# The attention stage of a fused attention and MoE kernel: its instructions in a hand-written order per pair of heads

## The chip, the cores and the metric

The program runs on 1 core of one Trainium2 chip, in one launch. The metric is the device time of one execution in microseconds (us), here the median of 3 runs; smaller is better.

## What is computed

Attention with a decay, then a mixture of experts with one expert per token, then a gated MLP:

```python
# attention: q, k, v are (4, 8, 576, 64), f is (4, 8, 576)
scores = scale * np.matmul(q, k.transpose(0, 1, 3, 2))
cum = np.cumsum(np.log(np.clip(f, 0.0001, 1.0)), axis=-1)
decay = cum[:, :, :, None] - cum[:, :, None, :]
scores = np.where(causal, -1000000000.0, scores + decay)
attn = np.exp(scores - np.max(scores, axis=-1, keepdims=True))
attn = attn / (np.sum(attn, axis=-1, keepdims=True) + 1e-09)
x = np.matmul(attn, v)                       # -> 2304 tokens of 512
# routing and experts: 8 experts, 512 -> 1024 -> 512
e_idx = np.argmax(x @ w_gate + modality_bias[modality_id], axis=1)
out[mask] = gate_w[mask, None] * (np.maximum(x[mask] @ w1[e], 0.0) @ w2[e])
# gated MLP: 512 -> 1536 -> 512
y = (1.0 / (1.0 + np.exp(-(out @ w_gate2))) * (out @ w_val)) @ w_out
```

## The kernel before

Attention comes first and fills about the first 360 us; behind it follow the end of the routing, the experts and the gated MLP, whose code the change leaves as it is (products at L953 and L963, L1288 and L1376).

**Pairs.** Attention works on 16 pairs: one head of two batches side by side, the two batches j = 0, 1 in the two halves of the arrays. The 576 rows of a head are five blocks of rows, b = 0 (64 rows) and 1 to 4 (128 rows), of which a block needs only the columns up to its diagonal.

**Steps.** `run` goes through steps n = 0 to 17. Step n works on four pairs at once:
- pair n: its scores. QA to QD are the products q·k (L202, in PSUM tiles `s`); T0 to T4 (Ta and Tb are halves of T4) add the decay from `dec` to them, write the sum to the SBUF tiles `sc` and keep each row's minimum in `mn` (L209 on VectorE, DVE for short); E0 to E4 take the exponential in place on ScalarE (ACT) and leave row sums in `sm` (L218).
- pair n−1: X, Y and Z transpose its probabilities on TensorE (PE) into PSUM banks of the tag `t` (L235). A bank holds four to six 128x128 blocks and is copied out whole to `px`, `py` or `pz`, for j = 1 by DVE (L239), for j = 0 by ACT (L241). A0 to A2 and M are the products with v (L291) into `o` and `m`, which are copied to `ot`. `sums` adds 1e-9 to the row sums on GpSimd (POOL, L279, tile `r`) and takes their reciprocal on DVE (L280).
- pair n−2: U takes from a list the two parts of `normalise`: `ot` is transposed back by a product with `iw` (L323, L328; it carries the gate's columns along), scaled by `r` on DVE (L331, L510), and the logits are added up on POOL (L511).
- pair n+1: U also takes `prep`, the transposes of q and k (L174, L180, copied out at L169 by ACT and L167 by DVE); `mask` builds the decay tile `dec` on POOL, ten tensor_scalars (L153) and ten affine_selects (L157). The loads of v for pair n+1, and of q, k and the decay row (`cum`) for pair n+2, are issued on the SP queue.

The banks `t` are two (`TB = 2`) and serve X, Y, Z, `prep` and `normalise`, 12 fills a step; `s` has four, `o` and `m` one each, `dec` two pairs.

**What sets the order.** A tile scheduler reorders the whole program by its own estimates; the string `ORDER` sets only in which order the steps are handed to it. L takes an item from a list of late work (routing of the first half of the tokens, sending `x` to HBM), one or two per step.

Of the kernel before, what the change touches and what calls it, by code (L numbers as in the profile page):

```python
# [20 lines left out]
P = 128  # L21
# [35 lines left out]
    return slice(0, P) if b else slice(D * j, D * (j + 1))  # L57


class Attention:  # L60


    NV = 3
    ORDER = "QA T1 Ta X QB Tb T0 U Y E1 E4 A0 L QC T3 Z E3 A1 U E0 QD T2 U E2 A2 M U U L"

    def __init__(self, tc, ctx, top, ro, ps, q, k, v, f):
        nc = self.nc = tc.nc
# [35 lines left out]
        self.load_v(0)  # L103
        nc.vector.tensor_copy(self.swp[:, 0:64], ident[:, 64:128])
        nc.vector.tensor_copy(self.swp[:, 64:128], ident[:, 0:64])

    def spare(self, tag, shape, dt):

# [36 lines left out]
    def mask(self, n):  # L145

        nc = self.nc
        d = self.dec[n] = [self.pd.tile([P, DW], F32, tag="dec", name="dec") for j in range(2)]
        for b in (1, 4, 0, 3, 2):
            for j, c in enumerate(self.cum[n]):  # L150
                r, m = lanes(b, j), P if b else D
                t = d[j]
                nc.gpsimd.tensor_scalar(  # L153
                    t[r, DO[b]:DO[b] + W[b]], c[r, 0:W[b]], -1.0, c[r, R0[b]:R0[b] + 1], ALU.mult, ALU.add
                )
                sl = t[r, DO[b] + W[b] - m:DO[b] + W[b]]
                nc.gpsimd.affine_select(sl, sl, [[-1, m]], ALU.is_ge, NEG, base=0, channel_multiplier=1)  # L157
        del self.cum[n]

    def prep(self, n):  # L160

        nc, ident = self.nc, self.ident
        qk = self.qk[n] = [self.pt.tile([P, S], F32, tag=t, name=t) for t in ("qT", "qk")]

        def put(w, dst, src):
            if w:
                nc.vector.tensor_copy(dst, src)  # L167
            else:
                nc.scalar.activation(dst, src, AF.Copy, scale=0.125)  # L169

        def main(w):
            t, raw = self.bank(), self.raw[n][w]
            for c in range(4):
                nc.tensor.transpose(t[:, c * P:(c + 1) * P], raw[:, c].rearrange("p j d -> p (j d)"), ident)  # L174
            put(w, qk[w][:, 0:512], t)

        def rest():
            t = self.bank((P, 2, D))
            for w in range(2):
                nc.tensor.transpose(  # L180
                    t[:, w], self.raw[n][w][0:64, 4].rearrange("p j d -> p (j d)"), ident[0:64, 0:64]
                )
            for w in range(2):
                put(w, qk[w][:, 512:576], t[:, w])

        return [lambda: main(0), lambda: main(1), rest]

    def scores(self, n):
        nc = self.nc
        s, d = self.sc[n % 2], self.dec.pop(n)  # L190
        mn = [self.wk.tile([P, 6], F32, tag="mn", name="mn", bufs=4) for j in range(2)]
        q, k = self.qk[n]
        sm = self.sm[n] = self.wk.tile([P, 9], F32, tag="sm", name="sm", bufs=2)
        t = {}

        def qk(items):
# [20 lines left out]
                so, c = s[j][r, SO[b]:SO[b] + W[b]], 2 * (b - 1) + j if b else 8  # L217
                nc.scalar.activation(so, so, AF.Exp, bias=mn[j][r, b:b + 1], scale=-1.0, accum_out=sm[r, c:c + 1])  # L218

        return qk, add_max, exp  # L220

    def probs(self, n):

# [16 lines left out]
            else:  # L240
                nc.scalar.activation(dst, src, AF.Copy)  # L241

        def x():
            for j in range(2):
                t = self.bank()
                for b in (4, 3, 2, 1):
                    tr(j, t[:, P * (b - 1):P * b], b, 0)
                put(j, p[j][0], t)

        def y():  # L250
            for j in range(2):
                t = self.bank()
                tr(j, t[:, 384:512], 0, 0, j == 0)
                tr(j, t[:, 0:128], 1, 1, True)
                for b in (2, 3, 4):
                    tr(j, t[:, 64 + P * (b - 2):64 + P * (b - 1)], b, 1)
                put(j, p[j][1], t)

        def z():
            for j in range(2):  # L260
                t = self.bank()
                tr(j, t[:, 0:128], 3, 3, True)
                tr(j, t[:, 64:192], 4, 3)
                tr(j, t[:, 192:320], 2, 2, True)
                tr(j, t[:, 256:384], 3, 2)
                tr(j, t[:, 384:512], 4, 2)
                put(j, p[j][2][:, 0:512], t)
            t = self.bank((P, 2, P))
            for j in range(2):
                tr(j, t[:, j], 4, 4, True)  # L270
            nc.vector.tensor_copy(pz[:, :, 512:576], t[:, :, 0:64])

        return x, y, z

    def sums(self, n):
        nc, sm = self.nc, self.sm.pop(n)
        r = self.r[n] = self.wk.tile([P, 9, 1], F32, tag="r", name="r", bufs=3)
        rf = r.rearrange("p t o -> p (t o)")
        nc.gpsimd.tensor_scalar(rf, sm, 1e-9, None, ALU.add)  # L279
        nc.vector.reciprocal(rf, rf)  # L280

    def values(self, n):

# [15 lines left out]

        def c2():  # L300
            mm(o[0][:, 192:512], 2, 2, 192, 512, False, False)
            mm(o[0][:, 320:512], 3, 2, 0, 192, False, False)
            mm(o[0][:, 448:512], 4, 2, 512, 576, False, True)
            nc.vector.tensor_copy(ot[:, 64:S], o[0])

        def first():
            om = self.ps.tile([P, 64], F32, tag="m", name="m", bufs=1)
            mm(om, 0, 1, 448, 512, True, True)
            nc.vector.tensor_copy(ot[:, 0:64], om)

        return c0, c1, c2, first

    def normalise(self, n):
        nc = self.nc
# [4 lines left out]
        def part(b0, k, last):  # L319
# [6 lines left out]
                )  # L326
            for j in range(2 * last):
                nc.tensor.matmul(t[D * j:D * (j + 1), 2 * k], ot[:, 0:D], iw[:, h, j], start=True, stop=True)  # L328
            m, t0 = 2 * k + last, 2 * (b0 - 1)
            g, rs = HT * bp + t0, r[:, t0:t0 + m]  # L330
            nc.vector.tensor_tensor(  # L331
# [1 line left out]
            )  # L333
            self.ro.logits(slice(g, g + m), h, t[:, 0:m, D:], rs)

        return [lambda: part(1, 3, 0), lambda: part(4, 1, 1)]

    def run(self):
        N = len(self.pairs)
        nop = lambda *a: None  # L340
        pend, late = [], []

        def unit(todo):
            if todo:
                todo.pop(0)()

        for u in self.prep(0):
            u()
        self.load_dec(0)
        self.mask(0)  # L350
        self.load_qk(1)
        self.load_dec(1)
        n = 0
        while n < N + 2 or pend or late:
            if n == 0:
                self.ro.load()
            if n == 1:
                self.ro.biases()
            if n == 4:
                self.ro.tables()  # L360
            if 2 <= n < N + 2:
                m = n - 2
                pend += self.normalise(m)
            if n + 1 < N:
                self.load_v(n + 1)
                pend[:0] = self.prep(n + 1)
                self.mask(n + 1)
            if n + 2 < N:
                self.load_qk(n + 2)
                self.load_dec(n + 2)  # L370
            qk = add_max = exp = nop
            if n < N:
                qk, add_max, exp = self.scores(n)
            px = py = pz = nop
            av = (nop,) * 4
            if 1 <= n <= N:
                px, py, pz = self.probs(n - 1)
                av = self.values(n - 1)
                self.sums(n - 1)

            step = {
                "QA": lambda: qk([(4, 0, 256, 0), (1, 0, 192, 256)]),
                "QB": lambda: qk([(4, 256, 320, 0), (0, 0, 64, 320)]),
                "QC": lambda: qk([(3, 0, 448, 0)]),
                "QD": lambda: qk([(2, 0, 320, 0)]),
                "Ta": lambda: add_max(4, 0, 256), "Tb": lambda: add_max(4, 256, 576),
                "T0": lambda: add_max(0), "T1": lambda: add_max(1), "T2": lambda: add_max(2), "T3": lambda: add_max(3),
                "E0": lambda: exp(0), "E1": lambda: exp(1), "E2": lambda: exp(2), "E3": lambda: exp(3),
                "E4": lambda: exp(4),
                "X": px, "Y": py, "Z": pz, "A0": av[0], "A1": av[1], "A2": av[2], "M": av[3],  # L390
                "U": lambda: unit(pend), "L": lambda: unit(late),
            }
            for key in self.ORDER.split():
                step[key]()
            if 2 <= n < N + 2 and n % 2:
                late += self.ro.columns(*self.pairs[n - 2])
            n += 1


class Routing:  # L400
# [33 lines left out]
        self.tc = wp.tile([P, 2 * E + 1], F32, tag="tc", name="tc")  # L434
        self.given = mid, w_gate, bias

    def load(self):
        nc, (mid, w_gate, bias) = self.nc, self.given
        nc.gpsimd.memset(self.iw, 0.0)
        for i in range(2):  # L440
            a = slice(D * i, D * (i + 1))
            nc.vector.tensor_copy(self.iw[a, :, i, 0:D], self.ident[a, a].unsqueeze(1).to_broadcast([D, H, D]))
            nc.sync.dma_start(self.iw[a, :, i, D:], w_gate.rearrange("(h p) e -> p h e", p=D))
        for bp in range(2):
            ids = mid.bitcast(I32).rearrange("(b s two) -> b s two", b=B, two=2)
# [1035 lines left out]
def decayed_attention_top1_moe_gated_kernel(  # L1481
# [15 lines left out]
    with ExitStack() as c1:  # L1497
# [4 lines left out]
        with ExitStack() as c0:  # L1502
            with ExitStack() as top:
                att = Attention(tc, c0, top, ro, ps, q, k, v, f)
                att.run()
            ro_t = c1.enter_context(tc.tile_pool(name="ro_t", bufs=1, side="right", reuse_waits="tile"))
            ex.begin(att)
            collect = ro.finish(ro_t, ps)
# [79 lines left out]
```

## Time and profile before

| what | value |
|---|---|
| median of 3 runs | 1054.45 us (1054.3 to 1055.09) |
| profiled execution | 1057.33 us, its span 1055.6 us |
| mean granted clock of TensorE | 0.961 |
| busy share of the span | PE 91%, DVE 67%, ACT 51%, POOL 21% |
| start of step 0's scores | 8.48 us |
| first operation of the second half's argmax (end of attention) | 360.60 us |

The span is the part of an execution that the profiler shows. The busy shares are means over stages with different limits; attention is the first third. The granted clock of TensorE is given in shares of 2.4 GHz; 0.5 is its lower level, 1.2 GHz.

### The profile page before, as it was taken

To read this page: it belongs to the slowest core of one execution; us is meant where nothing else is said; L and a number is where in the kernel's file an instruction comes from. 1 tells how busy PE (TensorE), PEld (TensorE's weight loads), DVE (VectorE), ACT (ScalarE), POOL (GpSimd) and SP (SyncE) were. 2 spreads that over 40 slices of the span, in tenths; PEclk is the share of its full clock that TensorE was granted. 3 is DMA by queue.
4 is the path that set the end of the run, shared out by engine and by line. 5 is a ranking of instruction groups with operands and counts; after the bars stand their busy time and mean duration, and the time that the engine had idled before them with its cause. 6 is when DMAs were issued, how large, how long until landed. Compare 5 with 4: busy or idle time off the path is not lost. (4 is left out here: it accounts for less than half of the span.)

```text
span 1055.6 us, 16303 instructions
## 1 busy us (share of the span) xinstructions
PE 959.2 (91%) x5423; PEld 774.2 (73%) x5423; DVE 705.4 (67%) x1744; ACT 533.4 (51%) x1155; POOL 222.7 (21%) x467
## 2 busy tenths in 40 slices
PE   6796788886789899999999999899999999999996
PEld 3463444443445688999999798789999899999995
DVE  4563434444645597999998747878866688876662
ACT  4443333333335155666667734555665555655452
POOL 6564333444334313111112000000020000200002
PEclk9898889889889999999999989999999999999999
DMA  6452422243621264684578464421332112321201
GB/s 139 119 130 67 103 71 57 68 112 80 193 69 41 48 198 147 220 313 161 170 239 292 157 244 135 146 80 60 120 140 80 60 61 79 111 71 65 76 21 60
DMA packets 118892, 126.69 MB, mean 120 GB/s; under 512 B 65744, under 2 KB 92880, under 8 KB 118800
## 3 DMA queue, kind: packets, MB, share of 16 engines
q1 hardware_dynamic: 114160, 110.87, 34.4%
q0 software_dynamic: 4640, 14.70, 4.1%
q8 instruction: 44, 0.72, 0.3%
q14 instruction: 48, 0.39, 0.1%
HBM read 127.03 MB, written 24.21 MB: 143 GB/s over the span
## 5 line engine op out<-in xcount | busy, mean ns | idle before, releaser
L1288 PE MATMUL g<-x,wc 128*128 128x384 f32 x1536 | 304.6, 340 | 10.0 <-ACT pc L1325 3.1
L1288 PEld LDWEIGHTS g<-x,wc 128*128 128x128 f32 x1536 | 276.3, 189 | 30.1 <-ACT pc L1325 4.4
L1376 PE MATMUL o<-wo,ah 128*128 128x512 f32 x648 | 184.5, 397 | 0.2 <-DVE ah L1313 0.2
L218 ACT ACTIVATE sc<-sc,mn 128x192 f32<-128x192 f32 (+4 forms) x160 | 88.8, 556 | 184.3 <-DVE mn L209 183.8
L1376 PEld LDWEIGHTS o<-wo,ah 128*128 128x128 f32 x648 | 118.0, 188 | 11.6 <-DVE ah L1313 1.0
L153 POOL TENSOR_SCALAR dec<-cum 128x192 f32<-128x192 f32 (+4 forms) x160 | 84.2, 536 | 145.8 <-DVE mn L209 133.2
L1384 POOL DMA_INDIRECT out_dram<-os,tok x18 | 18.4, 1024 | 423.2 <-ACT os L1383 417.7
L887 DVE TENSOR_TENSOR wl<-ws,wh 128x1024 fp32r<-128x1024 f32 x80 | 97.0, 1215 | 0.0
L881 ACT ACTIVATE wh<-ws 128x1024 fp32r<-128x1024 f32 x80 | 84.6, 1060 | 18.6 <-PE y L963 18.6
L1312 ACT ACTIVATE ah<-s 128x384 fp32r<-128x384 f32 x72 | 37.9, 526 | 99.7 <-DVE s L1311 99.7
L235 PE MATMUL t<-swp,sc 128*128 128x128 f32 x144 | 38.9, 322 | 53.9 <-DVE px L239 53.2
L209 DVE CUSTOM_DVE_ANT_0 sc<-s,dec 128x192 f32<-128x192 f32 (+4 forms) x160 | 61.5, 417 | 36.0 <-PE s L202 26.0
L235 PEld LDWEIGHTS t<-swp,sc 128*128 128x128 f32 x144 | 19.9, 157 | 79.7 <-DVE px L239 55.8
L953 PE MATMUL h<-xh,wh 128*128 128x256 f32 x256 | 73.6, 288 | 0.0
L953 PE MATMUL h<-xh,wl 128*128 128x256 f32 x256 | 72.5, 283 | 0.7 <-DVE wl L887 0.7
L202 PE MATMUL s<-qk,qT 64*128 64x320 f32 (+4 forms) x384 | 69.4, 452 | 3.7 <-DVE mn L209 3.1
L953 PE MATMUL h<-xl,wh 128*128 128x256 f32 x256 | 72.4, 283 | 0.3 <-DVE xl L908 0.3
L235 PE MATMUL t<-ident,sc 128*128 128x128 f32 x336 | 64.5, 306 | 1.1 <-ACT px L241 0.7
L933 POOL DMA_INDIRECT rows_by_expert<-ys,dst x20 | 23.9, 1195 | 195.4 <-ACT hh L923 106.0
L235 PEld LDWEIGHTS t<-ident,sc 128*128 128x128 f32 x336 | 45.9, 157 | 25.1 <-ACT sc L218 19.3
L1325 ACT ACTIVATE pc<-g 128x384 f32<-128x384 f32 x96 | 46.4, 483 | 31.1 <-PE g L1288 31.0
L1171 DVE TENSOR_TENSOR wc<-wf,wc 128x512 fp32r<-128x512 f32 x72 | 40.7, 568 | 30.7 <-ACT wc L1168 30.7
(266 smaller groups left out, 1844.2 us busy)
## 6 DMA issues: line engine op xcount, KB each, us to landing
ws<-in_moe_w_dram SPq DMA_DIRECT2D x80, 512.0 KB
wf<-wd SPq DMA_DIRECT2D x36, 512.0 KB
cum<-drow SPq DMA_DIRECT2D x32, 288.0 KB
wd<-dec SPq DMA_DIRECT2D x18, 512.0 KB
wof<-wd SPq DMA_DIRECT2D x18, 512.0 KB
raw<-in_moe_w_gate_dram SPq DMA_DIRECT2D x12, 512.0 KB
raw<-in_moe_w_val_dram SPq DMA_DIRECT2D x12, 512.0 KB
raw<-in_moe_w_out_dram SPq DMA_DIRECT2D x12, 512.0 KB
```

The lines of the kernel that those rows point to most:

```text
L153: nc.gpsimd.tensor_scalar(t[r, DO[b]:DO[b] + W[b]], c[r, 0:W[b]], -1.0, c[r, R0[b]:R0[b] + 1], ALU.mult, ALU.add)
L202: nc.tensor.matmul(out[r, o:o + w], q[a, rows], k[a, c0:c0 + w], start=True, stop=True)
L209: nc.vector.tensor_tensor_reduce(s[j][r, SO[b] + c0:SO[b] + e], t[j, b, c0][:, 0:e - c0], d[j][r, DO[b] + c0:DO[b] + e], -1.0, mn[j][r, 5: ...
L218: nc.scalar.activation(so, so, AF.Exp, bias=mn[j][r, b:b + 1], scale=-1.0, accum_out=sm[r, c:c + 1])
L235: nc.tensor.transpose(dst, s[j][:, SO[b] + P * c:SO[b] + P * (c + 1)], self.swp if low else self.ident)
L881: self.nc.scalar.activation(hi, self.wraw(u, k), AF.Copy)
L887: ins = eng.tensor_tensor(lo, self.wraw(u, k), hi.bitcast(F32), ALU.subtract)
L953: nc.tensor.matmul(t, a[:, c, cs], b[:, c, :], start=(n == 0), stop=(n == 3 * KD - 1))
L1171: V(t["w"][:, 1, to], of(), t["w"][:, 0, to].bitcast(F32), ALU.subtract)
L1288: self.nc.tensor.matmul(t, p[:, c, :], q[:, c, :], start=(first and n == 0), stop=(n == total - 1), skip_group_check=not first)
L1325: nc.scalar.activation(c, t, AF.Copy)
L1376: nc.tensor.matmul(o[0], x[:, cs], y[:, r, :], start=(o[1] == 0 and k == 0), stop=(o[1] == 2 * self.NP - 1 and k == 2))
```

## The change

The attention stage now runs inside `tc.manual_schedule()`: every instruction of it stands where `run` calls it. `ORDER` becomes a list in which filling a bank (upper case: X0, Y1, PQ, N1) and copying it out (lower case: x0, y1, pq, n1) are steps of their own; a generator with a `yield` between the two halves does that. The same work stands in it, with these differences:
- `sums(n − 1)` is called ahead of `mask(n + 1)`, so POOL's operation on `r` stands ahead of that mask; the reciprocal is the step rc. `sm` has three buffers, not two.
- The copy of `o` (128x512) goes from DVE to ACT, that of the last bank of Z (128x2x64) too; the copies of `o` and `m` are made in the next step.
- A0 (both halves of the product with `px`) and A1 (with `py`) are steps that follow whole fills; A2 is cut in A2 and A3.
- The ten tensor_scalars of mask(0) are on DVE, the decay's load for pair 0 is issued ahead of `prep(0)`, and the set-up of `iw` is done when the tiles are made. `tables()`, which the scheduler had put at the start, stays in step 4.
- The two L stand at the end of a step.

```diff
+def two(names, run):
+
+    return dict.fromkeys(names.split(), lambda: next(run, None))
...
-    ORDER = "QA T1 Ta X QB Tb T0 U Y E1 E4 A0 L QC T3 Z E3 A1 U E0 QD T2 U E2 A2 M U U L"
+    ORDER = (
+        "X0 X1 ot x0 om x1 QA Y0 Y1 T1 y0 Ta E1 QB A0 y1 Tb E4 T0 rc N1 Z0 n1 z0 QC E0 Z1 T3 N2 z1 QD A1 n2 T2 E3 "
+        "L0 PQ l0 A2 pq E2 PK PR A3 M pk pr L L"
+    )
...
-                nc.gpsimd.tensor_scalar(
+                (nc.gpsimd if n else nc.vector).tensor_scalar(
...
-        sm = self.sm[n] = self.wk.tile([P, 9], F32, tag="sm", name="sm", bufs=2)
+        sm = self.sm[n] = self.wk.tile([P, 9], F32, tag="sm", name="sm", bufs=3)
...
-        def x():
-            for j in range(2):
-                t = self.bank()
-                for b in (4, 3, 2, 1):
-                    tr(j, t[:, P * (b - 1):P * b], b, 0)
-                put(j, p[j][0], t)
...
+        def x(j):
+            t = self.bank()
+            for b in (4, 1, 3, 2):
+                tr(j, t[:, P * (b - 1):P * b], b, 0)
+            yield
+            put(j, p[j][0], t)
...
-            nc.vector.tensor_copy(pz[:, :, 512:576], t[:, :, 0:64])
...
+            nc.scalar.activation(pz[:, :, 512:576], t[:, :, 0:64], AF.Copy)
...
-        nc.vector.reciprocal(rf, rf)
+        return {"rc": lambda: nc.vector.reciprocal(rf, rf)}
...
-            nc.vector.tensor_copy(ot[:, 64:S], o[0])
...
+        def main():
+            nc.scalar.activation(ot[:, 64:S], o[0], AF.Copy)
...
+            step = {"L": lambda: late.pop(0)() if late else None}
+            if 1 <= n <= N:
+                step |= self.sums(n - 1)
...
             for key in self.ORDER.split():
-                step[key]()
+                if key in step:
+                    step[key]()
...
-                att.run()
+                with tc.manual_schedule():
+                    att.run()
```

How the order of the instructions moves, at three places of a step in the middle of attention.

POOL before, one step's queue: `dec` rows are the mask of pair n+1, `lg` the logits of pair n−2, `r` the row sums of pair n−1.

```order
L153 TENSOR_SCALAR dec<-cum 128x192
L153 TENSOR_SCALAR dec<-cum 128x576
L157 AFFINE_SELECT dec<-dec 128x128
L153 TENSOR_SCALAR dec<-cum 128x192
...
L153 TENSOR_SCALAR dec<-cum 128x320 x2
L511 TENSOR_TENSOR lg<-lt,lg 128x24
L157 AFFINE_SELECT dec<-dec 128x128 x2
L279 TENSOR_SCALAR r<-sm 128x9
```

POOL of the changed kernel, the same queue (L162, L166, L530 and L302 are the old L153, L157, L511 and L279):

```order
L530 TENSOR_TENSOR lg<-lt,lg 128x48
L530 TENSOR_TENSOR lg<-lt,lg 128x24
L302 TENSOR_SCALAR r<-sm 128x9
L162 TENSOR_SCALAR dec<-cum 128x192
L166 AFFINE_SELECT dec<-dec 128x128
L162 TENSOR_SCALAR dec<-cum 128x192
L166 AFFINE_SELECT dec<-dec 128x128
```

The operation on `r` went from the end of a mask to its head, and each affine_select now stands right behind the tensor_scalar whose result it takes.

DVE before, where a step begins (`ot`, `x`, `lt` end the step before; ISA rows are T1, then Ta):

```order
L304 COPY ot<-o 128x512
L309 COPY ot<-m 128x64
L331 TENSOR_TENSOR x<-t,r 128x6x64
L510 TENSOR_TENSOR lt<-t,r 128x48
L331 TENSOR_TENSOR x<-t,r 128x3x64
L510 TENSOR_TENSOR lt<-t,r 128x24
L209 ISA sc,mn<-s,dec 128x192
L209 ISA mn 128x1
L280 RECIPROCAL r<-r 128x9
...
L209 ISA sc,mn<-s,dec 128x256
L209 ISA mn 128x1
L239 COPY px_2129<-t 128x512
```

DVE of the changed kernel, from the same place (L220, L255, L303, L338 are the old L209, L239, L280, L309):

```order
L338 COPY ot<-m 128x64
L255 COPY px_2337<-t 128x512
L220 ISA sc,mn<-s,dec 128x192
...
L255 COPY py_2338<-t 128x512
L220 ISA sc,mn<-s,dec,mn 128x320
L220 ISA mn 128x1
...
L303 RECIPROCAL r<-r 128x9
L361 TENSOR_TENSOR x<-t,r 128x6x64
L529 TENSOR_TENSOR lt<-t,r 128x48
```

The reciprocal stood ahead of the copies of px and py and now stands behind both, and the copy of `o` is gone from DVE.

PE before, around the product with px (`sc` rows transpose probabilities, `swp` and `ident` are the two constant matrices for it):

```order
L235 MATMUL t<-swp,sc 128x128 x2
L235 MATMUL t<-ident,sc 128x128 x3
L291 MATMUL o<-px_2766,vr_126 64x512
L235 MATMUL t<-ident,sc 128x128
L235 MATMUL t<-swp,sc 128x128
L235 MATMUL t<-ident,sc 128x128 x3
L291 MATMUL o<-px_2768,vr_126 64x512
L202 MATMUL s<-qk,qT 128x448 x2
```

PE of the changed kernel, the same part (L251, L314, L213 are the old L235, L291, L202):

```order
L251 MATMUL t<-swp,sc 128x128 x2
L251 MATMUL t<-ident,sc 128x128 x4
L251 MATMUL t<-swp,sc 128x128
L251 MATMUL t<-ident,sc 128x128 x3
L213 MATMUL s<-qk,qT 128x320 x2
L213 MATMUL s<-qk,qT 64x64 x2
L314 MATMUL o<-px_2994,vr_124 64x512
L314 MATMUL o<-px_2996,vr_124 64x512
```

The two halves of the product with px stood apart, with a fill of a bank between them; now they stand side by side. The same holds for py.

## Rows read from the trace of the kernel before

**Rows 1.** Windows of steps: us, busy PE, PEld, DVE, ACT, POOL, clock, DMA share, GB/s.
```profile
45.36:60.70 15.34, 15.34 (x104) 8.98 (x100) 9.83 (x36) 8.02 (x25) 11.45 (x31) 1.00 0.43 110
...
143.68:166.52 22.84, 18.00 (x103) 9.97 (x100) 9.84 (x38) 8.24 (x25) 8.35 (x24) 0.85 0.25 65
...
211.02:324.99 113.97, 89.50 (x515) 49.32 (x512) 55.58 (x226) 41.76 (x128) 45.54 (x121) 0.88 0.42 114
```

**Rows 2.** PE's timeline: start, us; first product of steps 1, 4, 15.
```profile
23.18 1.61 PE L202 MATMUL s<-qk,qT 64*128 64x256 f32 x8 [0.15 <-ACT qT L169]
...
76.01 1.03 PE L202 MATMUL s<-qk,qT 64*128 64x256 f32 x8
...
324.99 1.03 PE L202 MATMUL s<-qk,qT 64*128 64x256 f32 x8
```

**Rows 3.** Timeline of all engines around the start of step 8.
```profile
164.41 1.16 POOL L153 TENSOR_SCALAR dec<-cum 128x192 f32<-128x192 f32 x2 [14.07 <-DVE mn L209]
...
172.94 0.24 POOL L279 TENSOR_SCALAR r<-sm 128x9 f32<-128x9 f32 x1
173.22 0.22 DVE L280 RECIPROCAL r<-r 128x9 f32<-128x9 f32 x1 [5.27 <-POOL r L279]
...
174.26 0.69 DVE L239 COPY px<-t 128x512 f32<-128x512 f32 x1
...
175.00 0.69 PE L235 MATMUL t<-swp,sc 128*128 128x128 f32 x2 [4.84 <-DVE px L239]
...
176.26 1.92 PE L291 MATMUL o<-px,vr 128*64 128x512 f32 x2
```

**Rows 4.** Who waited for tile r, 100 to 330 us: us, times.
```profile
  DVE r L280: 52.6, 11
```

**Rows 5.** PE's timeline, products with v in an undisturbed step.
```profile
51.17 1.07 PE L291 MATMUL o<-px,vr 128*64 128x512 f32 x2
52.17 1.02 PE L202 MATMUL s<-qk,qT 64*128 64x448 f32 x4
...
58.00 1.20 PE L291 MATMUL o<-pz,vr 128*64 128x320 f32 x12
...
59.03 0.29 PE L291 MATMUL m<-py,vr 128*64 128x64 f32 x4
```

**Rows 6.** Timeline: a bank's fill, and its copy.
```profile
56.57 0.66 PE L174 MATMUL t<-ident,kr 128*128 128x128 f32 x4
...
57.26 0.69 DVE L167 COPY qk<-t 128x512 f32<-128x512 f32 x1 [1.19 <-PE t L174]
```

**Rows 7.** Groups by form: busy time, mean ns of one | idle before.
```profile
L304 DVE COPY ot<-o 128x512 f32<-128x512 f32 x16 | 10.9, 682 | 1.3 <-PE o L291 1.3
L241 ACT ACTIVATE px<-t 128x512 f32<-128x512 f32 x16 | 9.3, 579 | 3.0 <-PE t L235 3.0
L271 DVE COPY pz<-t 128x128 f32<-128x128 f32 x16 | 4.6, 290 | 7.6 <-PE t L235 7.6
```

**Rows 8.** POOL's timeline: a select, and what is next.
```profile
26.74 0.24 POOL L157 TENSOR_SCALAR_AFFINE_SELECT dec<-dec 64x64 f32<-64x64 f32 x1
27.08 0.64 POOL L153 TENSOR_SCALAR dec<-cum 128x448 f32<-128x448 f32 x1
```

**Rows 9.** Timeline of the start.
```profile
3.60 0.58 DVE L99 TENSOR_SCALAR x<-x 32x576 f32<-32x576 f32 x1
...
13.74 1.16 POOL L153 TENSOR_SCALAR dec<-cum 128x192 f32<-128x192 f32 x2 [8.74 <-DMA cum<-drow]
...
15.18 0.36 DVE L209 CUSTOM_DVE_ANT_0 sc<-s,dec 128x192 f32<-128x192 f32 x1 [6.66 <-POOL dec L157]
```

**Rows 10.** Timeline of the end of attention.
```profile
353.23 2.06 POOL L879 TENSOR_SCALAR esc<-eraw 128x1024 fp32r<-128x1024 f32 x2 [5.75 <-PE t L235]
...
360.09 0.48 POOL L511 TENSOR_TENSOR lg<-lt,lg 128x48 f32<-128x48 f32 x2
...
360.60 0.23 DVE L536 TENSOR_REDUCE lm<-lg 128x9 f32<-128x72 f32 x1 [1.92 <-POOL lg L511]
```

More of the change, by code (lines that the diff above doesn't have):

```diff
@@ L105, in __init__ @@
         nc.vector.tensor_copy(self.swp[:, 64:128], ident[:, 0:64])
+        ro.unit()
     def spare(self, tag, shape, dt):
@@ L182, in rest @@
                 )
+            yield
             for w in range(2):
                 put(w, qk[w][:, 512:576], t[:, w])
-        return [lambda: main(0), lambda: main(1), rest]
+        return two("PQ pq", main(0)) | two("PK pk", main(1)) | two("PR pr", rest())
     def scores(self, n):
@@ L218, in exp @@
                 nc.scalar.activation(so, so, AF.Exp, bias=mn[j][r, b:b + 1], scale=-1.0, accum_out=sm[r, c:c + 1])
-        return qk, add_max, exp
+        return {
+            "QA": lambda: qk([(4, 0, 256, 0), (1, 0, 192, 256)]), "QB": lambda: qk([(4, 256, 320, 0), (0, 0, 64, 320)]),
+            "QC": lambda: qk([(3, 0, 448, 0)]), "QD": lambda: qk([(2, 0, 320, 0)]),
+            "Ta": lambda: add_max(4, 0, 256), "Tb": lambda: add_max(4, 256, 576),
+            **{f"T{b}": lambda b=b: add_max(b) for b in range(4)}, **{f"E{b}": lambda b=b: exp(b) for b in range(5)},
+        }
     def probs(self, n):
@@ L241, in put, with y, z, last @@
                 nc.scalar.activation(dst, src, AF.Copy)
-        def x():
-            for j in range(2):
-                t = self.bank()
-                for b in (4, 3, 2, 1):
-                    tr(j, t[:, P * (b - 1):P * b], b, 0)
-                put(j, p[j][0], t)
[L250 to L267, printed above, removed]
+        def x(j):
+            t = self.bank()
+            for b in (4, 1, 3, 2):
+                tr(j, t[:, P * (b - 1):P * b], b, 0)
+            yield
+            put(j, p[j][0], t)
+        def y(j):
+            t = self.bank()
+            tr(j, t[:, 384:512], 0, 0, j == 0)
+            tr(j, t[:, 0:128], 1, 1, True)
+            for b in (2, 3, 4):
+                tr(j, t[:, 64 + P * (b - 2):64 + P * (b - 1)], b, 1)
+            yield
+            put(j, p[j][1], t)
+        def z(j):
+            t = self.bank()
+            tr(j, t[:, 0:128], 3, 3, True)
+            tr(j, t[:, 64:192], 4, 3)
+            tr(j, t[:, 192:320], 2, 2, True)
+            tr(j, t[:, 256:384], 3, 2)
+            tr(j, t[:, 384:512], 4, 2)
+            yield
+            put(j, p[j][2][:, 0:512], t)
+        def last():
             t = self.bank((P, 2, P))
@@ L270, in z @@
                 tr(j, t[:, j], 4, 4, True)
-            nc.vector.tensor_copy(pz[:, :, 512:576], t[:, :, 0:64])
-        return x, y, z
+            yield
+            nc.scalar.activation(pz[:, :, 512:576], t[:, :, 0:64], AF.Copy)
+        out = two("L0 l0", last())
+        for j in range(2):
+            for a, run in (("X", x), ("Y", y), ("Z", z)):
+                out |= two(f"{a}{j} {a.lower()}{j}", run(j))
+        return out
     def sums(self, n):
@@ L301, in c2, with c3, rest @@
             mm(o[0][:, 192:512], 2, 2, 192, 512, False, False)
+        def c3():
             mm(o[0][:, 320:512], 3, 2, 0, 192, False, False)
             mm(o[0][:, 448:512], 4, 2, 512, 576, False, True)
-            nc.vector.tensor_copy(ot[:, 64:S], o[0])
         def first():
[L307 to L311, printed above, removed]
+            o.append(self.ps.tile([P, 64], F32, tag="m", name="m", bufs=1))
+            mm(o[1], 0, 1, 448, 512, True, True)
+        def main():
+            nc.scalar.activation(ot[:, 64:S], o[0], AF.Copy)
+        def rest():
+            nc.vector.tensor_copy(ot[:, 0:64], o[1])
+        return {"A0": c0, "A1": c1, "A2": c2, "A3": c3, "M": first}, {"ot": main, "om": rest}
     def normalise(self, n):
@@ L328, in part @@
                 nc.tensor.matmul(t[D * j:D * (j + 1), 2 * k], ot[:, 0:D], iw[:, h, j], start=True, stop=True)
+            yield
             m, t0 = 2 * k + last, 2 * (b0 - 1)
@@ L334, in part @@
             self.ro.logits(slice(g, g + m), h, t[:, 0:m, D:], rs)
-        return [lambda: part(1, 3, 0), lambda: part(4, 1, 1)]
+        return two("N1 n1", part(1, 3, 0)) | two("N2 n2", part(4, 1, 1))
     def run(self):
         N = len(self.pairs)
[L340 to L348, printed above, removed]
+        late, outs = [], {}
         self.load_dec(0)
+        for f in self.prep(0).values():
+            f()
         self.mask(0)
@@ L353, in run @@
         n = 0
-        while n < N + 2 or pend or late:
+        while n < N + 2 or late:
+            step = {"L": lambda: late.pop(0)() if late else None}
+            if 1 <= n <= N:
+                step |= self.sums(n - 1)
             if n == 0:
@@ L360, in run @@
                 self.ro.tables()
-            if 2 <= n < N + 2:
-                m = n - 2
-                pend += self.normalise(m)
             if n + 1 < N:
                 self.load_v(n + 1)
-                pend[:0] = self.prep(n + 1)
+                step |= self.prep(n + 1)
                 self.mask(n + 1)
@@ L370, in run @@
                 self.load_dec(n + 2)
-            qk = add_max = exp = nop
             if n < N:
-                qk, add_max, exp = self.scores(n)
-            px = py = pz = nop
-            av = (nop,) * 4
-            if 1 <= n <= N:
[L377 to L392, printed above, removed]
+                step |= self.scores(n)
+            step |= outs
+            outs = {}
+            if 2 <= n < N + 2:
+                step |= self.normalise(n - 2)
+            if 1 <= n <= N:
+                step |= self.probs(n - 1)
+                now, outs = self.values(n - 1)
+                step |= now
             for key in self.ORDER.split():
-                step[key]()
+                if key in step:
+                    step[key]()
             if 2 <= n < N + 2 and n % 2:
@@ L435, in __init__, with unit @@
         self.given = mid, w_gate, bias
-    def load(self):
-        nc, (mid, w_gate, bias) = self.nc, self.given
+    def unit(self):
+        nc = self.nc
         nc.gpsimd.memset(self.iw, 0.0)
@@ L442, in load @@
             nc.vector.tensor_copy(self.iw[a, :, i, 0:D], self.ident[a, a].unsqueeze(1).to_broadcast([D, H, D]))
+    def load(self):
+        nc, (mid, w_gate, bias) = self.nc, self.given
+        for i in range(2):
+            a = slice(D * i, D * (i + 1))
             nc.sync.dma_start(self.iw[a, :, i, D:], w_gate.rearrange("(h p) e -> p h e", p=D))
```

## The prediction

> **What bounds the kernel now.** I read the windows first, cut at the first product of each step. Two kinds of steps show. In the undisturbed one PE is busy for all of its 15.34 us at clock 1.00; in a later one the same work takes 22.84 us, PE is busy for 18.00 of them and its mean clock is 0.85 [rows 1]. DVE, ACT and POOL have 9.8, 8.2 and 8.4 us of work there, so none of them is full. Steps 2 and 3 are of the first kind (45.36 to 76.01 us), and from 76.01 to 324.99 there are eleven of the second: 248.98 / 11 = 22.63 us each [rows 2]. The excess over 15.3 is 7.3 us a step.
>
> The timeline around the start of step 8 shows where it comes from [rows 3]. POOL gets its `dec` buffers back at 164.41 and runs a whole mask; its operation on `r` stands behind it and starts at 172.94. DVE's queue holds the reciprocal of that `r` ahead of the copy of px, so DVE sat idle for 5.27 us until 173.22, px was copied at 174.26, and PE, whose next fill needs that bank, stood still for 4.84 us until 175.00. The view of the tile `r` counts this wait eleven times in the loop, 52.6 us, 4.8 us a step [rows 4]. Behind the gap PE is slow: the product with px takes 1.92 us [rows 3] against 1.07 in the undisturbed step [rows 5], which is the lower of the two clock levels (1.2 GHz). The 0.85 mean says the same: 15% of 22.84 us is 3.4 us of lost clock, part of it in the gap, the rest some 2 us of longer work. 4.8 and 2 to 2.5 make up the 7.3.
>
> So the loop is bound by one wait in a circle POOL, DVE, PE, with PE's work as the floor below it.
>
> **The change part by part.**
>
> *Reciprocal out of the way.* POOL's operation on `r` now stands ahead of the mask, and the reciprocal behind T0, behind the copies of px and py. The wait of 4.8 us goes, and with it the gap that costs the clock: −7.3 us a step, down to 15.3. What is late next is PE's own work.
>
> *Products side by side.* The halves of the products with px and py stood apart, with a fill between them. One half of px took 1.00 us (51.17 to 52.17), and py 448/512 of that by its columns, 0.9: 2 x 1.0 + 2 x 0.9 = 3.8 us a step. Halves that stand side by side run at the same time: 576 columns of pz and py on both halves took 58.00 to 59.03, 1.03 us [rows 5]. By columns that is 0.92 for px and 0.80 for py, 1.7 us together, and I allow 0.2 for the changes between shapes. Saving 3.8 − 1.7 − 0.2 = 1.9 us; the floor is 13.4 to 13.5 us. Bounds: nothing gained (15.3) and all of it (13.4).
>
> *Copies moved.* DVE loses 0.68 (`ot`) and 0.29 (last of pz), 9.84 − 0.97 = 8.9 us; ACT takes some 0.58 and 0.25 by the copies it already makes [rows 7], 8.24 + 0.83 = 9.1 us. Both lie under 13.5.
>
> *Fixed hand-offs.* Twelve fills a step go through two banks, so a bank's round may last 13.5 / 6 = 2.25 us before PE waits. A fill of four took from 56.57 and its copy 57.26 to 57.95 [rows 6], a round of 1.4 us, and a fill of five or six takes 0.2 to 0.5 more. That leaves 0.35 to 0.85 us a round, less than a pair of T or E operations can take. In a hand-written order a late copy delays all that stands behind it. I take 0.8 us a step for it, which is four of the twelve fills late by 0.2 us; bounds 0 and 3. The step I forecast is 13.5 + 0.8 = 14.3 us.
>
> *POOL.* It has 8.35 us of work in a step, plus 0.5 at most in others, and a mask is now ten pairs in which the affine_select needs the result just written. One such hand-over on POOL shows as 27.08 − 26.98 = 0.10 us [rows 8]. Twenty of them give 8.8 + 2 = 10.8 us, hidden under 14.3. It would bind from (14.3 − 8.8) / 10 = 0.55 us a pair.
>
> *SP's queue.* The loads keep their places relative to the steps; steps at 15.3 us had a DMA share of 0.43 and no wait for one [rows 1], and 14.3 raises that to 0.46. Nothing.
>
> *Start.* mask(0) began at 13.74 when `cum` landed, and T1 at 15.18, beside POOL's work [rows 9]. On DVE ten tensor_scalars come first; by 0.58 us for 576 columns [rows 9] the 3,200 columns of a mask are 3.2 us. The tables of POOL leave the start but nobody waited for them. `cum` is issued a little earlier: T1 moves to about 13.6 + 3.2 = 16.8, and the first fill X0 of step 1 from 23.18 [rows 2] to about 25.0, a loss of 1.8; bounds 0 and 4.
>
> The Trainium skill, "SBUF — State Buffer", section "Who interferes with whom", says that a tensor_scalar on VectorE can take both ports of the pair it shares with GpSimd and then blocks that engine for the whole instruction. No run shown here has the two side by side in this way; by that rule the selects of mask(0) would wait for DVE's operations, at most another 3 us once, and the forecast would be 962.
>
> *Late items.* Steps 10 to 14 hold routing work besides: DVE is busy for 55.58 us there against 5 x 9.84 = 49.2 in plain steps [rows 1], 6.4 us, in chains with hand-overs to PE and ACT between them. Before, they lay in gaps; now they end a step, and its next X0 and x1 queue behind them. Chains run longer than their work, and part lies under PE's. I take 10 us in all; bounds 3 and 14.
>
> *End.* From the first product of step 15 to the first operation of the second argmax were 360.60 − 324.99 = 35.61 us [rows 2, 10]. Now it is one step (14.3) and the tail: in step 16 the last fill for weights' scaling on POOL comes about 7.9 us after X0, and from there POOL has the 7.4 us that it had from 353.23 to 360.60 [rows 10], with 0.4 for hops: 15.7. Together 30.0, a gain of 5.6; bounds 0 and 8.
>
> *Sum.* Step 1 was 45.36 − 23.18 = 22.18 us, now 14.3: 7.9. Steps 2 and 3: 2 x 1.0 = 2.0. Eleven steps: 11 x (22.63 − 14.3) = 91.6. Start −1.8, late items −10, end +5.6. In all 95.3 us: the argmax starts at 265.3 instead of 360.60. The rest, 1055.6 − 360.6 = 695.0 us, has the same instructions and keeps its length. The span becomes 960.3, the profiled execution 1057.33 − 95.3 = 962.0. That execution lay 2.9 above the median of the runs, so on their footing 1054.45 − 95.3 = **959 us**.
>
> **The rivals.**
>
> *A. The step stays at 15.3 to 16.5.* The wait goes, but what the pairing saves is eaten by late copies: DVE or ACT stands in T or E when a bank is full. For it speaks the short slack (0.35 us against T operations of 0.6 us in pairs); against it that DVE and ACT are under 70% busy. 15 x 1.0 to 15 x 2.2 more than forecast: 974 to 992. "TensorEngine Tiling (Array Packing)" of the Trainium skill, section "PSUM Bottleneck", says that tiling makes TensorE faster but not the emptying of PSUM, which is this case; no run shown here decides it.
>
> *B. At the floor.* Every hand-off fits, the step is 13.5 and the late items lie under PE's work: 12 and 10 us less, 937.
>
> *C. POOL binds.* If a dependent pair on POOL costs 1 us, not 0.2, a mask takes 18.8 us with the rest and the step follows it: 15 x 3.7 to 5.7 more, 1015 to 1045. The short gap [rows 8] speaks against it.
>
> *D. Slower than before.* A fixed order can make a new circle: a copy placed behind E work that waits for T, that waits for the products behind the next fill. Each step has six rounds for each bank. The gain is gone when 25.0 + 15 x step + 10 + 15.7 reaches 360.6, at a step of 20.7 us or a round of 20.7 / 6 = 3.4 us. At rounds of 3.6 to 4.0 us the step is 21.6 to 24, the argmax comes 14 to 50 us late, and the time is 1068 to 1105. Against it: rounds take 1.4 to 1.9 us [rows 6], and the order as it stands puts every copy within a few operations of its fill.
>
> That the change doesn't do what it says is excluded: the order of the instructions shows `r` ahead of the mask, the halves side by side, and `ot` off DVE.
>
> **How the numbers follow.** The forecast's own case (step 13.5 to 15.1) has 0.62, and by itself 943 to 975. A has 0.22, B 0.08, C 0.05, D 0.03. The range 940 to 988 takes in the first, most of A and what lies between B and the first; left out are C, D, half of B and the end of A. About 0.2% (2 us) is what a measurement of this kernel can tell from no change. All cases but D end well over 0.2% faster, so faster has 0.96, same 0.01 (a D that just misses), slower 0.03.
>
> **What would show it.** In the changed profile: no wait of the reciprocal on POOL's `r` over 0.5 us; PE's clock at 1.00 through attention, and its busy share near the whole step; products with px at 0.9 to 1.0 us for both halves; steps of 13.5 to 15.1 us; the argmax at about 265 us. PE waiting for a copy of DVE or ACT over 1 us a step would be A; POOL without idle time would be C; a clock that falls again in every step would be D. Were the stages behind the argmax longer than 695 us, the sum would fail outside attention.

## The result

The changed kernel takes **945.37 us** (median of 4 runs, 944.73 to 947.71) against 1054.38 us, a ratio of 0.897 (95% interval 0.895 to 0.899): 109 us faster. Its profiled execution took 945.15 us, its span is 943.4 us. The forecast was 959 us, within 940 to 988.

The windows of the changed kernel (columns as in [rows 1]) over one step, and over the steps 11 to 14 that carry most of the late items:

```profile
91.99:105.56 13.57, 13.57 (x104) 8.46 (x100) 8.92 (x35) 9.12 (x27) 8.74 (x24) 1.00 0.78 188
...
159.80:219.10 59.30, 55.59 (x419) 34.29 (x414) 43.70 (x178) 36.79 (x110) 37.24 (x98) 1.00 0.71 182
```

PE is busy for the whole of the first, at clock 1.00: 13.57 us where [rows 1] had 22.84. DVE and ACT have the 8.9 and 9.1 us that the prediction gave them. PE's timeline, first product of steps 1, 2, 6 and 7, and DVE's first operation of the second argmax:

```profile
25.91 1.03 PE L213 MATMUL s<-qk,qT 64*128 64x256 f32 x8
38.71 1.03 PE L213 MATMUL s<-qk,qT 64*128 64x256 f32 x8
...
93.01 1.03 PE L213 MATMUL s<-qk,qT 64*128 64x256 f32 x8
106.58 1.03 PE L213 MATMUL s<-qk,qT 64*128 64x256 f32 x8
...
248.44 0.23 DVE L555 TENSOR_REDUCE lm<-lg 128x9 f32<-128x72 f32 x1 [3.28 <-POOL lg L530]
```

Attention ends at 248.44 instead of 360.60 [rows 10], 112.2 us earlier, and what follows takes 943.4 − 248.4 = 695.0 us as before. So all of the gain lies in attention. The timeline of one step answers to [rows 3]:

```profile
96.21 1.08 PE L314 MATMUL o<-px,vr 128*64 128x512 f32 x4
...
97.78 0.21 DVE L303 RECIPROCAL r<-r 128x9 f32<-128x9 f32 x1
...
105.19 0.24 POOL L302 TENSOR_SCALAR r<-sm 128x9 f32<-128x9 f32 x1 [3.00 <-ACT sc L229]
...
105.53 0.43 POOL L162 TENSOR_SCALAR dec<-cum 128x192 f32<-128x192 f32 x1
```

The operation on `r` at 105.19 serves the next step, whose reciprocal comes 13.57 us behind the one at 97.78, at 111.35: it is 6.2 us early, the mask starts behind it, and no wait is noted at the reciprocal. Both halves of the product with px take 1.08 us together, where one half took 1.07 [rows 5].

### The profile page after: what moved, and what is told of

The parts are those of the page before. It is cut to its first block, busy times and chain, and to the rows that moved or that the text cites. A ratio compares the mean times of both kernels' runs of the same rounds, so it can differ in the third digit from the quotient of the medians.

```text
span 943.4 us, 16290 instructions
## 1 busy us (share of the span) xinstructions
PE 898.4 (95%) x5423; PEld 754.1 (80%) x5423; DVE 695.9 (74%) x1722; ACT 547.2 (58%) x1187; POOL 225.9 (24%) x457
## 5 line engine op out<-in xcount | busy, mean ns | idle before, releaser
L229 ACT ACTIVATE sc<-sc,mn 128x192 f32<-128x192 f32 (+4 forms) x160 | 88.2, 553 | 24.3 <-DVE mn L220 23.8
L162 POOL TENSOR_SCALAR dec<-cum 128x192 f32<-128x192 f32 (+4 forms) x150 | 79.8, 532 | 9.6 <-DMA cum<-drow 5.5
L220 DVE CUSTOM_DVE_ANT_0 sc<-s,dec 128x192 f32<-128x192 f32 (+4 forms) x160 | 61.1, 419 | 16.3 <-PE s L213 14.3
L213 PE MATMUL s<-qk,qT 64*128 64x320 f32 (+4 forms) x384 | 65.6, 440 | 7.0 <-DVE mn L220 6.5
L251 PE MATMUL t<-ident,sc 128*128 128x128 f32 x336 | 54.8, 276 | 3.8 <-DVE px L255 1.7
L1323 ACT ACTIVATE sg<-sg 128x384 f32<-128x384 f32 x48 | 25.2, 525 | 45.2 <-DVE sg L1353 18.8
L166 POOL TENSOR_SCALAR_AFFINE_SELECT dec<-dec 128x128 f32<-128x128 f32 (+1 forms) x160 | 45.6, 287 | 23.3 <-DVE dec L162 12.1
L972 PEld LDWEIGHTS h<-xl,wh 128*128 128x128 f32 x256 | 49.4, 193 | 2.0 <-DVE xl L927 0.5
```

Of the source, the lines that this page charges most:

```text
L162: (nc.gpsimd if n else nc.vector).tensor_scalar(t[r, DO[b]:DO[b] + W[b]], c[r, 0:W[b]], -1.0, c[r, R0[b]:R0[b] + 1], ALU.mult, ALU.add)
L213: nc.tensor.matmul(out[r, o:o + w], q[a, rows], k[a, c0:c0 + w], start=True, stop=True)
L220: nc.vector.tensor_tensor_reduce(s[j][r, SO[b] + c0:SO[b] + e], t[j, b, c0][:, 0:e - c0], d[j][r, DO[b] + c0:DO[b] + e], -1.0, mn[j][r, 5: ...
L251: nc.tensor.transpose(dst, s[j][:, SO[b] + P * c:SO[b] + P * (c + 1)], self.swp if low else self.ident)
L972: nc.tensor.matmul(t, a[:, c, cs], b[:, c, :], start=(n == 0), stop=(n == 3 * KD - 1))
```

## The experiments

Each is compared with the kernel before on the same chip in the same runs, so ratios compare across groups better than times. The last two columns are read from the profiled execution.

| kernel | median us | ratio, 95% interval | step in the loop, us | argmax at, us |
|---|---|---|---|---|
| changed kernel | 945.37 | 0.8973 (0.8953 to 0.8992) | 13.57 | 248.44 |
| e1 sums first, scheduler | 992.88 | 0.9408 (0.9380 to 0.9437) | 16.48 | 297.02 |
| e2 `r` behind the mask | 969.23 | 0.9195 (0.9177 to 0.9213) | 13.57 | 271.29 |
| e3 the same, rc early | 1058.83 | 1.0044 (1.0029 to 1.0060) | 20.50 | 359.19 |
| e4 rc early alone | 952.95 | 0.9042 (0.9026 to 0.9058) | 13.57 | 254.11 |
| e5 halves apart | 974.93 | 0.9261 (0.9246 to 0.9276) | 15.46 | 277.92 |
| e6 scheduler orders | 961.01 | 0.9116 (0.9099 to 0.9133) | 14.61 | 263.23 |
| e7 copies on DVE | 948.07 | 0.9003 (0.8988 to 0.9018) | 13.57 | 249.62 |
| e8 x1 behind T1 | 959.10 | 0.9103 (0.9088 to 0.9119) | 14.61 | 261.25 |
| e9 mask(0) on POOL | 949.27 | 0.8973 (0.8948 to 0.8997) | 13.57 | 252.36 |
| e10 one L inside | 944.62 | 0.8934 (0.8914 to 0.8954) | 13.57 | 246.73 |
| e11 fewer shapes | 945.66 | 0.8946 (0.8930 to 0.8962) | 13.45 | 246.79 |
| e12 both | 942.42 | 0.8925 (0.8906 to 0.8945) | 13.45 | 245.34 |

**The circle: e1 to e4.** My theory is that the step of before was one closed circle: POOL's mask, `r` behind it, the reciprocal, DVE's queue from there to T2, which gives `dec` back to POOL. The rival is that the fixed order as such brings the gain.

e1 is the kernel before with one call moved:

```diff
+            if 1 <= n <= N:
+                self.sums(n - 1)
             if n == 0:
                 self.ro.load()
...
                 av = self.values(n - 1)
-                self.sums(n - 1)
```

> The kernel before with one line moved: the call of sums ahead of mask, the scheduler free to order. It puts the operation on r behind five operations of the mask instead of behind all twenty, and the reciprocal behind the copy of o. Circle theory (the step lasts as long as POOL's part of the mask ahead of r, then DVE's queue from the reciprocal to T2, which gives the decay tiles back to the mask): 2 to 3 us on POOL and about 14 on DVE, a step of 15.3 to 17.5 instead of 22.6, time 970 to 998. Rival (the fixed order as such gives the gain, the wait is only a symptom that turns up elsewhere): steps above 20, time over 1030.

e2 is the changed kernel with the call of sums set behind that of mask; e3 the same with the list's rc moved:

```diff
-            if 1 <= n <= N:
-                step |= self.sums(n - 1)
...
                 self.mask(n + 1)
+            if 1 <= n <= N:
+                step |= self.sums(n - 1)
...
-"X0 X1 ot x0 om x1 QA Y0 Y1 T1 y0 Ta E1 QB A0 y1 Tb E4 T0 rc N1 ...
+"X0 X1 ot x0 om rc x1 QA Y0 Y1 T1 y0 Ta E1 QB A0 y1 Tb E4 T0 N1 ...
```

> The changed kernel with the operation on r behind the mask on POOL again, the reciprocal late as it is. Circle theory: the mask (about 10.4 us) starts at the end of T2, and from the reciprocal to the end of the next T2 DVE has 4.8 us: 15.4 us a step instead of 13.57, 15 steps: about 973, with a wait of about 2 us of the reciprocal for r in each step. Rival (what matters is where r stands on POOL alone): the whole wait comes back, 4 to 5 us a step and the clock with it, over 1020. Second rival (the place on POOL does not matter): 945.

> As the kernel with r behind the mask, and the reciprocal ahead of the copy of px, as it stood before. Circle theory: 10.4 us on POOL and then about 10 us of DVE from the reciprocal to the end of T2: 20.5 us a step or more, with TensorE's clock falling again in each; 1050 to 1080. Rival (the place on POOL alone): the same time as with the reciprocal late.

e4 has the list of e3 and leaves sums ahead of mask.

> The changed kernel with the reciprocal alone moved, ahead of the copy of px; r stays ahead of the mask. Circle theory: r is ready 0.4 us ahead of the step's first copy, so there is no circle and no wait: 945, within 3. Rival (the reciprocal's place on DVE is what brought the gain): over 960.

e3 takes back the whole gain with two moves: 1058.83 us, 0.4% slower than before, though all the rest of the hand-written order stands. Its window over one step and its timeline show the picture of [rows 3] again:

```profile
178.67:199.17 20.50, 16.24 (x102) 9.46 (x101) 8.77 (x35) 9.24 (x28) 8.85 (x24) 0.83 0.29 72
```

```profile
183.57 0.24 POOL L302 TENSOR_SCALAR r<-sm 128x9 f32<-128x9 f32 x1
183.84 0.21 DVE L303 RECIPROCAL r<-r 128x9 f32<-128x9 f32 x1 [5.83 <-POOL r L302]
...
184.66 0.47 PE L251 MATMUL t<-ident,sc 128*128 128x128 f32 x1 [4.26 <-DVE px L255]
...
187.69 1.97 PE L314 MATMUL o<-px,vr 128*64 128x512 f32 x4
```

The reciprocal waits 5.83 us, PE 4.26 us, and the product with px takes 1.97 us at the lower clock instead of 1.08. It is not the kernel before in every part: the step is 20.5 us and not 22.6, steps 1 and 14 are longer (28.2 and 26.1 us against 22.2 each), and of the 1057.2 us of its span 698.0 lie behind the argmax, 3.0 more than before. Why these differ is not shown.

In e4, with `r` first, the early reciprocal costs 7.6 us by the medians, 5.7 at the argmax: the loop's step is 13.57 us, and it waits for `r` three times (10.1 us in the view of the tile), in steps 1, 2 and 15. I had expected no cost, so that was missed; but no step in the middle of the loop waits. With `r` behind the mask the same early place costs 89.6 us (e3 less e2).

e2 came out near its number for another reason. I had expected 15.4 us in each step; the step is 13.57. The rows of its loop:

```profile
140.25 0.24 POOL L302 TENSOR_SCALAR r<-sm 128x9 f32<-128x9 f32 x1
140.53 0.21 DVE L303 RECIPROCAL r<-r 128x9 f32<-128x9 f32 x1 [0.43 <-POOL r L302]
...
142.11 0.62 DVE L220 CUSTOM_DVE_ANT_0 sc<-s,dec 128x448 f32<-128x448 f32 x1 [0.68 <-PE s L213]
...
144.75 0.43 POOL L162 TENSOR_SCALAR dec<-cum 128x192 f32<-128x192 f32 x1 [0.19 <-DVE mn L220]
...
153.82 0.24 POOL L302 TENSOR_SCALAR r<-sm 128x9 f32<-128x9 f32 x1
```

From the reciprocal to the mask's start are 4.2 us, and the mask up to the next `r` takes 153.82 − 144.75 = 9.07 us, not the 10.4 that I took. With the hop to DVE (0.28) these parts add up to the step, as parts of one round must, so the sum alone says nothing. What tells is DVE's wait for PE inside it: 0.68 us. Without that wait the circle would be some 12.9 us (an estimate from these rows), 0.7 below PE's 13.57. The 24 us are single delays that are longer than this room, in the view of its waits for `r` over attention:

```profile
DVE r L303 <- POOL r L302: 24.0, 10, 11.1
...
POOL am L608 <- DVE hot L603: 5.7, 1, 5.7
```

11.1 us come in step 1 (23.8 us), where the mask waits 4.65 us for its `cum` and `r` stands behind all of it. Step 4, with the tables of POOL ahead of the mask, takes 17.2 us, and step 14, with a late item of POOL (`am`) there, 23.2.

e1, under the scheduler and with one call moved, has a step of 16.48 us, clock 1.00:

```profile
141.74:158.22 16.48, 15.34 (x103) 8.98 (x100) 9.75 (x37) 8.02 (x25) 8.32 (x24) 1.00 0.34 90
```

PE's 15.34 us are those of [rows 1], and 1.1 us of gaps are left. They are the old wait, shorter: `r` now stands 3.1 us behind the mask's start, and DVE still waits for it with the rest of its queue behind.

```profile
143.02 0.22 DVE L280 RECIPROCAL r<-r 128x9 f32<-128x9 f32 x1 [1.71 <-POOL r L279]
...
143.91 1.06 PE L235 MATMUL t<-ident,sc 128*128 128x128 f32 x8 [1.14 <-DVE lt L511]
```

So of the 109 us that line gives 62, with no hand-written order, and the rival, that only the fixed order brings the gain, falls.

**The floor: e5.** B0 and B1 are the second halves of A0 and A1; N1 alone stands between those of px.

```diff
-... y1 Tb E4 T0 rc N1 Z0 n1 z0 QC E0 Z1 T3 N2 z1 QD A1 n2 ...
+... y1 Tb E4 T0 rc N1 B0 Z0 n1 z0 QC E0 Z1 T3 N2 z1 A1 QD B1 n2 ...
```

> The changed kernel with the two halves of the products with px set apart by N1 and a fill between, and those with py by QD. PE is busy all along in its step of 13.57 us, so what is added on PE is added to the step: by the rows of before, halves apart cost 3.8 us and side by side 1.7, so 15.6 us a step, 15 to 16 steps, +31 to +34 us: 976 to 980, clock at 1.00. Rival (halves side by side bring nothing, the step shrank for other reasons): 945, within 3.

```profile
87.17:102.63 15.46, 15.46 (x101) 8.77 (x100) 9.01 (x35) 9.13 (x28) 8.82 (x24) 1.00 0.38 96
```

15.46 us, PE busy throughout: 1.89 us more, the 1.9 us of the prediction, and 29.6 us in time, a little less than the 31 to 34 expected of this run. Side by side is worth what it was priced at, because PE is the bound.

**The hand-offs: e6, e7, e8.** e6 drops `with tc.manual_schedule()`; e7 makes the copies of `o` and of the last bank of Z with `nc.vector.tensor_copy`; e8 sets one copy late:

```diff
-"X0 X1 ot x0 om x1 QA Y0 Y1 T1 y0 ...
+"X0 X1 ot x0 om QA Y0 T1 x1 Y1 y0 ...
```

> The changed kernel without manual_schedule: the same code and list, the tile scheduler orders. It puts r behind six operations of the mask and the reciprocal ahead of the copies of prep's banks at the end of the step. If what counts is only that the circle over POOL is open, 945 to 950. Circle theory: the reciprocal there waits for E2 and for the first part of the mask, and the copy of kr behind it is late for PE: 14.5 to 16.5 us a step, 960 to 990.

> The changed kernel with the copy of o and the last copy of pz back on DVE. PE theory: both fall into places where DVE stands idle in the step (0.76 us ahead of x1, 2.0 us ahead of pq's copy), so PE sees them no later: 945, within 3. Rival (DVE's load was part of the gain): 0.3 us a step or more, 950 and over.

> The changed kernel with one copy late on purpose: x1 behind T1 on DVE, so Y1's bank comes free later. From the trace x1 would end 2.0 us later than it does, and the fill Y1, which has 0.76 us of room, would wait 1.2 us: 14.8 us a step, +18 us, 963; up to 970 if the clock falls in the gap. Rival (the hand-offs have room for more than 1 us): 945 to 950.

The scheduler with the same list gives 14.61 us a step, at the lower end of what I expected. DVE's and PE's timelines show why:

```profile
111.46 0.22 DVE L303 RECIPROCAL r<-r 128x9 f32<-128x9 f32 x1 [3.08 <-POOL r L302]
111.59 0.76 DVE L176 COPY qk<-t 128x512 f32<-128x512 f32 x2
...
112.28 1.09 PE L251 MATMUL t<-ident,sc 128*128 128x128 f32 x8 [0.97 <-DVE qk L176]
```

It set the reciprocal ahead of the copies of `qk`, and PE waits 0.97 us for one of them. The late copy is again the wait for `r`: POOL comes to it 3.1 us after the mask's start, and DVE stands idle for 3.08 us. In e8 DVE copies px late and PE waits 0.84 us; the step is 1.04 us longer, 13.7 us in time, somewhat less than the 18 expected:

```profile
101.01 0.69 DVE L255 COPY px<-t 128x512 f32<-128x512 f32 x1
...
101.84 0.30 PE L251 MATMUL t<-ident,sc 128*128 128x128 f32 x1 [0.84 <-DVE px L255]
```

e7 leaves the step at 13.57 us and its profiled execution took 945.15 us, that of the changed kernel. Its median is 2.7 us higher, at the very edge of what I expected, and its argmax 1.2 us later; the intervals of the two ratios overlap, so a gain from moving the copies is not shown; by the ends of the intervals it is 7 us at most.

By ratios, the call of `sums` (e1, 5.9% of the time before), the halves side by side (e5 against the changed kernel, 2.9%) and the hand-written order (e6 against it, 1.4%) come to 10.2 of the 10.3% gained. They start from different kernels, so that they add up so well shows only that nothing large is left over.

**Start and late items: e9 to e12.**

```diff
e9:  -(nc.gpsimd if n else nc.vector).tensor_scalar(
     +nc.gpsimd.tensor_scalar(
e10: -... E3 L0 PQ l0 A2 pq E2 PK PR A3 M pk pr L L
     +... E3 L0 PQ l0 L A2 pq E2 PK PR A3 M pk pr L
e11: -... z1 QD A1 n2 T2 E3 L0 PQ l0 A2 pq E2 PK PR A3 M pk pr L L
     +... z1 A1 QD n2 T2 E3 L0 PQ l0 pq PK PR A2 pk E2 A3 M pr L L
e12: the order of e11, with "l0 pq L PK" and one L at the end
```

> The changed kernel with the ten tensor_scalars of mask(0) on POOL again. From the trace of the changed kernel: POOL would need about 9 us for mask(0) from 13.3 us on, so T2 of step 0 would end at about 23.8 instead of 22.5, and all behind it 0.5 to 1.5 us later: 945.5 to 947. The forecast's own figure (first decay on DVE costs 1.8 us) would give 943.5. Either is at the edge of what can be told.

> The changed kernel with one of the two L moved from the step's end to behind l0, where DVE stands idle for 2.0 us ahead of pk. Late items add 5.0 us to three steps of the changed kernel (15.4, 15.2 and 15.1 us instead of 13.57). If they cost because they stand ahead of om and x1 on DVE: 2 to 4 us less, 941 to 943. Rival (they cost wherever they stand): 945.

> The changed kernel with QD behind A1, and PK and PR ahead of A2: three changes of PE's operand shape less in each step. If the step is nothing but PE's work and a change costs 0.1 to 0.2 us, 0.3 to 0.6 us a step less, less what PR waits for pq's copy: 936 to 942. Rival (a hand-off turns late: T2 behind QD, the fill PK behind l0, PR behind pq): 945 to 955.

> Both: fewer changes of shape, and one L behind pq. The sum of the two gains where they are independent: 933 to 940. Rival: a late item ahead of PK delays pk's copy and with it the next X0, 942 to 950.

e9's profiled execution is the slowest of its five. It starts step 1 0.8 us sooner (25.11 against 25.91) and then loses 4.7 us in it, because POOL comes to the first `r` at 31.77 instead of 28.14; attention ends 3.9 us later in its trace, more than the 0.5 to 1.5 expected. Its times spread over 945 to 953 us, and the ratio is that of the changed kernel, so it is not settled by time. e10 shortens the late items from 5.0 to 2.5 us by the trace, as expected; by the ratio it is 4 us faster, but its interval just meets that of the changed kernel. e11 saves 0.12 us a step, less than the 0.3 expected, and its 945.66 us miss the 936 to 942:

```profile
92.58:106.03 13.45, 13.35 (x102) 8.49 (x101) 9.11 (x35) 9.14 (x28) 8.80 (x24) 1.00 0.81 196
```

PE's work falls by 0.22 us, 0.07 for each of three changes of shape, and a wait of 0.1 appears. e12 is the fastest kernel of the study; its interval lies below that of the changed kernel, half a per cent, through ratios that were taken on different chips. At 942.42 us it missed the 933 to 940, and its trace shows the rival that was named for it: a late item ahead of PK delays a copy of `qk`, and the next X0 waits, so that one step takes 15.85 us:

```profile
202.25 1.09 PE L251 MATMUL t<-ident,sc 128*128 128x128 f32 x8 [2.33 <-DVE qk L176]
```

## Why the prediction was right

**The wait and what hung on it.** Right, and shown by undoing it (e3) and by opening it with one call (e1). Eleven waits for `r` are gone, the clock is 1.00 in every step from there on. The chain was read off one step of the trace, and it closes into a circle: its length is the mask plus DVE's queue behind the reciprocal, so the place of rc decides as much as the place of `r`.

**The side-by-side products.** 1.9 us a step forecast; e5 measured 1.89.

**The hand-offs are the term that was off most.** I took 0.8 us a step for late copies, "four of the twelve fills late by 0.2 us". In a plain step it is none: PE is busy for 13.57 of 13.57 us, the floor that I had put at 13.4 to 13.5. That is (14.3 − 13.57) x 15 = 11 of the 17 us by which attention ended sooner than forecast (248.4, not 265.3). The margin was a guess from the slack of a round; e8 shows what a copy that is really late costs, 1.04 us. Rival A took the rule "PSUM Bottleneck" of the Trainium skill's "TensorEngine Tiling (Array Packing)", that tiling speeds up TensorE but not the emptying of PSUM, as its mechanism; in this trace the emptying keeps up, with DVE and ACT busy for 8.92 and 9.12 us of 13.57 and no gap in PE's work.

**Late items** took 5.0 us, not 10: three steps of 15.37, 15.21 and 15.07 us, where DVE has an item ahead of om and x1 and PE waits for a copy that comes late by it. **End:** from X0 of step 16 to 248.44, 15.15 us, not 15.7, in the parts that were forecast: POOL's scaling of weights starts 8.0 us after X0 (241.25) and the argmax 7.2 us after that. **Start:** X0 of step 1 at 24.69, not 25.0. With 15 steps: 24.69 + 203.6 + 5.0 + 15.15 = 248.4.

```profile
233.29 1.26 PE L251 MATMUL t<-ident,sc 128*128 128x128 f32 x8 [0.97 <-DVE xl L927]
```

Two steps that are not plain cancel in this sum. Step 1 is 0.6 us shorter (24.69 to 37.69). Step 15 has no next pair to prepare, and yet takes 14.19 us (219.10 to 233.29): a late item's transposes take PE 1.09 us there, and X0 of step 16 waits 0.97 us behind it. So the late items cost somewhat more than 5.0 us.

**From the trace to the median.** By the trace the forecast was 16.9 us too long (962.0 against 945.15), by the medians 13.8. The difference is the 2.9 us by which the profiled execution of before lay over its median; that of the changed kernel lies 0.2 under its own, so taking the 2.9 off brought the forecast nearer by luck.

**POOL** was rated too slow. The prediction gave its work of a step 10.8 us; it takes 10.57, from `r` at 91.62 to the end of the last `lg` at 102.19, with 0.80 of waiting for DVE in it. It counted twenty hand-overs of 0.10 us, and [rows 8] shows one behind a 64x64 select, whose result the next operation does not need; two in a mask are of that kind. In the changed kernel a select waits 0.08 us for its tensor_scalar (91.95 + 0.42 to 92.45), and behind a 128x128 select no time passes (92.45 + 0.29 to 92.73). That changed nothing here, but a mask of 9.07 us, not the 10.4 expected for e2, is why e2 stays under PE's step.

**A reading.** The 576 columns of [rows 5] were taken as those of pz and py; they are pz's alone. The price per column is the same.

**Rival B** (13.5 us a step, all late items hidden, 937) had the step right; **D** could be made with two moves (e3), by another mechanism than the one I gave for it: no bank's round, but a reciprocal.

## What to carry to other kernels

When an engine waits in every iteration, follow the chain until it closes: the iteration is as long as the circle, and a small operation that stands behind a long one in one queue and ahead of a long one in the next is enough to close it. Moving it on either queue opens the circle; only opening it on both left room for single delays here (e2 lost 24 us to them, e4 7.6). Once PE is busy all along at full clock, the next gains are its own work, and a hand-written order is worth what the scheduler's late copies cost, here 1 us a step (e6), much less than the one call (e1).

## What the runs showed of the hardware

Gaps of PE of about 1 us in every step did not lower the granted clock: it is 1.00 in the steps of e1, e6 and e8 with 1.14, 0.97 and 0.84 us. The gap of 4.26 us in e3 did, and products took 1.97 us instead of 1.08 behind it.

In step 0 of the changed kernel POOL's selects ran beside DVE's tensor_scalars, and a select took 362 ns there, against 295 ns in the mean of 128 in the kernel before (groups by form: busy us, mean ns, idle before):

```profile
L166 POOL TENSOR_SCALAR_AFFINE_SELECT dec<-dec 128x128 f32<-128x128 f32 x9 | 3.0, 362 | 12.3 <-DVE dec L162 12.1
```

```profile
L157 POOL TENSOR_SCALAR_AFFINE_SELECT dec<-dec 128x128 f32<-128x128 f32 x128 | 35.6, 295 | 0.8
```

In e9, where POOL does both, the selects of the same mask take 294 ns. "SBUF — State Buffer" of the Trainium skill, "Who interferes with whom", says that a tensor_scalar on VectorE can run in a mode that uses the ports it shares with GpSimd, and that whichever of the two issues first then blocks the other for its whole instruction. The trace shows 0.6 us for nine selects, far from the 3 us that I had taken from the rule, and no run tells whether the ports or something else slowed them.
